# One-block sums over finished q and k rows, separate buffers for products and values, and softmax planned step by step

## The chip, the cores and the metric

The kernel runs on 1 core of one Trainium2 chip. The metric is the device time of one execution in microseconds, as the median of several runs.

## The reference, cut to what matters

With one sequence of 2048 positions and width 640, the output is x plus two branches of the same layernormed x: a local attention and a gated bilinear layer.

```python
xn = layernorm(x)                                   # no gain, eps 1e-5
# A: 32 heads of 20; each position sees itself and 7 earlier ones, 2 apart
qkv = xn @ wqkv                                     # q, k, v
logits[h, s, w] = q[h, s] . k[h, s - 2 * w] * 20 ** -0.5   # -1e9 where s < 2 * w
o[h, s] = sum_w softmax_w(logits)[h, s, w] * v[h, s - 2 * w]
A = o @ wo
# B
B = ((xn @ w_gate) * (xn @ w_up)) @ w_down          # inner width 1536
return x + A + B
```

Everything is bfloat16 in memory.

## The kernel before, in words

The 2048 positions are 16 tiles of 128, in 4 chunks of 512 (`CH` = 4 tiles each). The kernel is written as steps. `add(engine, cost, fn, deps, occ, after)` records a step with a planned cost; `Plan.order` then sorts all of them by list scheduling: among the steps that are ready on an engine it takes the one with the least latest-start time, and it moves the clock of that engine on by `occ`. The order that comes out is the order in which the instructions of each engine are issued. On the chip each engine works through its own queue strictly in that order and waits by semaphores. The plan's times are estimates written into the code by hand; on the chip nothing but the order is left of them.

For a chunk, the stages are:

- Layernorm of a tile: statistics on VectorE (DVE), the power on GpSimd (POOL), and the application on DVE, or from tile 8 on on ScalarE (ACT). The tile is transposed into `xnT`, from tile 4 on by a DMA transpose that is issued on SyncE's queue (SP, L353).
- `qk`: q and k of the chunk, transposed, by TensorE (PE, L419) and copied out of PSUM by ACT (L426). q and k have two buffers each, by chunk. A k tile has 14 columns in front, the last ones of the chunk before, which `halo` copies.
- `vproj`: v of each tile (L452), copied out by ACT and stored to a DRAM buffer `vD` by POOL's queue.
- `products` (L520): DVE multiplies q with the eight shifted k, in 8 instructions of 128x2560 for each chunk, in two halves of 256 positions. The 20 elements of a head lie on 4 partitions times 5 rows (`KT` = 5).
- `fold` (L496): DVE adds the 5 rows together. `LEVELS` = (1, 2, 3, 3) says how far in each chunk: with one level three rows are left, with two levels two, with three levels one. `logits` (L539) adds what is left over the 4 partitions on PE, with a small 0/1 matrix `Ek`: 12, 8, 4 and 4 matmuls for each half of the chunks 0 to 3. In this kernel the logits of both halves come after all products and folds of the chunk.
- The logits go out of PSUM by ACT (L555) and are transposed to `LT` by a DMA transpose on SP's queue (L562).
- `softmax`: one step `mx` on DVE (three maxima and a subtract, L581 to L585), the exponential on ACT (L590), and one step `nrm` on DVE (three sums, a reciprocal and a scale, L598 to L603), for each half.
- `load_v8` (L613): a DMA on SP's queue brings, for one tile, the eight shifted v rows of each position, 1280 KB. `av`: DVE multiplies them with the softmax (L638) and adds them in three tree instructions (L647, L651, L653) to `o`, which a DMA transpose on SP's queue (L660) turns into `oT`.
- `glu`: 24 groups of 5 matmuls (L680), ACT copies (L685) and a DVE product (L696) into `hT`.
- `down`: for each tile the matmuls over `hT` and `wd` (L740) and over `oT` and `wo` (L743), the copy out, and the store onto an output that already holds x. The first tile of a chunk does 10 of its 12 `hT` matmuls before it needs the last two.

PE gets the main matmuls in a written order (`pe_main`): for each chunk c the gate and up matmuls of c, `down` of c, then q, k and v of chunk c + 2. Only the logits groups are placed into it by the planner; they are marked urgent, and `margin` is the slack that the plan leaves between the last fold and them.

Products and v rows share one set of 5 buffers, tag `pv`. The order of the v loads on SP's queue is partly fixed in `load_v8`: in chunks 1 to 3 the second and third load of a chunk come behind the `LT` transposes of both halves (`SS`), and the first one behind the third product pair:

```python
order = [SPLAST[0]] if t < CH - 1 else [SS[2 * (t // CH) + 1]] if t % CH in (1, 2) else []
c, u = divmod(t, CH)
order.append(V8[t - 1] if u else PW[8 * c + 6])
```

Of the kernel before, what the change touches and what calls it, by code (L numbers as in the profile page):

```python
# [10 lines left out]
ALU = mybir.AluOpType  # L11
# [20 lines left out]
class Plan:  # L32


    LAG = 0.06
    INORDER = ("DVE", "PE", "ACT")
# [4 lines left out]
    def add(self, eng, cost, fn, deps=(), occ=None, after=(), kb=0):  # L41
        s = Step(eng, cost, fn, deps, occ, after)
        s.kb = kb
        s.idx = len(self.steps)
        self.steps.append(s)
        return s

    def order(self):
# [16 lines left out]
        while True:  # L65
            best = None
            for eng, items in ready.items():
                if not items:
                    continue
                f = free.get(eng, 0.0)  # L70
                t0 = max(f, min(r for r, _ in items))
                r, s = min((x for x in items if x[0] <= t0 + 1e-9), key=lambda x: (x[1].late, x[1].idx))
                if best is None or t0 < best[0]:
                    best = (t0, r, s)
            if best is None:
                break
            t0, r, s = best
            ready[s.eng].remove((r, s))
            s.start, s.end = t0, max(t0 + s.cost, s.floor)
            if s.kb:  # L80
                s.end = queue[s.eng] = max(t0 + 2.0, queue.get(s.eng, 0.0)) + s.kb / 340
                s.end = queue[s.eng] = max(s.end, s.floor)
            free[s.eng] = t0 + s.occ
            out.append(s)
            for t in s.succ:
                t.left -= 1
                if t.left == 0:
                    at = max(
                        d.start + d.occ if d in t.after else (d.start + d.occ if d.eng == t.eng and d.eng in self.INORDER else d.end + (0.0 if d.eng == t.eng else self.LAG) + t.margin)
                        for d in t.deps  # L90
                    )
                    ready.setdefault(t.eng, []).append((at, t))
# [5 lines left out]
def kernel(  # L98
# [296 lines left out]
    Q, Kk, LASTPW = {}, {}, {}  # L395
    HALOCP = {}

    def halo(c):
# [6 lines left out]
        if c == 0:  # L405
            HALOCP[c] = add("DVE", 0.1, fn)
        else:
            HALOCP[c] = add("ACT", 0.25, fn, [LASTPW.get(c - 2), *Kk[c - 1]])

    def qk(c, lo, n, rs=(0, 1)):  # L410
        for r in rs:
            for j in range(KT):
# [17 lines left out]
                mine = [WK if r else WQ, *[TX.get(t, TT[t]) for t in ts], LASTPW.get(c - 2)]  # L430
# [50 lines left out]
    PW, LL, LE, SS, DD, AA, O16, OE, V8, DT = {}, {}, {}, {}, {}, {}, {}, {}, {}, {}  # L481

    LEVELS = (1, 2, 3, 3)
    FOLDER = ('DVE', 'DVE', 'DVE', 'DVE')
    LEFT = (tuple(range(KT)), (0, 1, KT - 1), (0, KT - 1), (0,))
    HALVES = ((0, 2, 2, 4), (0, 1, 1, 2), (0, 1, KT - 1, KT))

    HS = CS // 2

    def fold(c, u):  # L490
        s = PW[8 * c + 2 * u + 1]
        for lo, hi, a, b in HALVES[: LEVELS[c]]:
            def fn(lo=lo, hi=hi, a=a, b=b):
                w = T["pw", c, u]
                if FOLDER[c] == "DVE":
                    nc.vector.tensor_tensor(w[:, :, lo:hi, :], w[:, :, lo:hi, :], w[:, :, a:b, :], ALU.add)  # L496
                else:
                    nc.gpsimd.dma_start(out=w[:, :, lo:hi, :], in_=w[:, :, a:b, :], accum_op=ALU.add)
            n = (hi - lo) * 4 * HS
            if FOLDER[c] == "DVE":  # L500
                s = add("DVE", 0.25 + n / 1920, fn, [s], occ=0.1 + n / 1920)
            else:
                s = add("POOL", 6.2, fn, [s], occ=1.2)
        return s

    def products(c, hf):
        for j in range(4):
# [15 lines left out]
            w = [LL.get(2 * c - 1), O16.get(4 * c - 4), O16.get(4 * c - 3), O16.get(4 * c - 2)][u]  # L523
            PW[m] = add("DVE", 1.48, mul, [*Q[c], *Kk[c], w], occ=1.395, after=[(FO[4 * c + 1] if i == 4 else PW.get(m - 1)) if i else V8.get(4 * c - 1)])
            if j % 2:
                FO[4 * c + u] = fold(c, u)
        LASTPW[c] = PW[m]
# [3 lines left out]
    def logits(c, g):  # L531
        n = 2 * c + g

        def lg():
            l = new(("lps", c, g), [P, 512], F32, "pl", 2, psum)
            left = LEFT[LEVELS[c]]
            for i in left:
                for j in range(4):
                    nc.tensor.matmul(l[H * j : H * (j + 1), :], lhsT=Ek[:], rhs=T["pw", c, 2 * g + j // 2][:, 2 * (j % 2) : 2 * (j % 2) + 2, i, :],  # L539
                                     start=(i == left[0]), stop=(i == left[-1]), tile_position=(0, H * j),  # L540
                                     skip_group_check=True)

        alone = not (g and c in PAIRED)
        took = 0.022 + 0.2195 * len(LEFT[LEVELS[c]]) + (0.19 if alone else 0.0)
# [30 lines left out]
    def softmax(c, hf):  # L575
        n = 2 * c + hf

        def mx():
            L4 = T["LT", n]
            m = sb.tile([P, 2, 4, H], BF, name="m", tag="m", bufs=1)  # L580
            nc.vector.tensor_tensor(m[:], L4[:, :, 0:4, :], L4[:, :, 4:8, :], ALU.max)  # L581
            nc.vector.tensor_tensor(m[:, :, 0:2, :], m[:, :, 0:2, :], m[:, :, 2:4, :], ALU.max)
            nc.vector.tensor_tensor(m[:, :, 0:1, :], m[:, :, 0:1, :], m[:, :, 1:2, :], ALU.max)
            d = new(("d", n), [P, 2, W, H], F32, "d", 2)
            nc.vector.tensor_tensor(d[:], L4[:], m[:, :, 0:1, :].to_broadcast([P, 2, W, H]), ALU.subtract)  # L585

        DD[n] = add("DVE", 1.52, mx, [SS[n], AA.get(n - 2)], occ=1.43)
# [7 lines left out]
        def nrm():  # L595
            d = T["d", n]
            s = sb.tile([P, 2, 4, H], F32, name="s", tag="s", bufs=1)
            nc.vector.tensor_tensor(s[:], d[:, :, 0:4, :], d[:, :, 4:8, :], ALU.add)  # L598
            nc.vector.tensor_tensor(s[:, :, 0:2, :], s[:, :, 0:2, :], s[:, :, 2:4, :], ALU.add)
            nc.vector.tensor_tensor(s[:, :, 0:1, :], s[:, :, 0:1, :], s[:, :, 1:2, :], ALU.add)  # L600
            nc.vector.reciprocal(s[:, :, 0, :], s[:, :, 0, :])
            a = new(("a", n), [P, 2, W, H], BF, "a", 2)
            nc.vector.tensor_tensor(a[:], d[:], s[:, :, 0:1, :].to_broadcast([P, 2, W, H]), ALU.mult)  # L603

        AA[n] = add("DVE", 2.33, nrm, [e, O16.get(2 * n - 3)], occ=2.24)

    def load_v8(t):
        def fn():
            v = new(("v8", t), [P, W, D], BF, "pv", 5)
# [21 lines left out]
    def av(t):  # L631
# [17 lines left out]
        def tree2():  # L649
            v = T["v8", t]  # L650
            nc.vector.tensor_tensor(v[:, 0:2, :], v[:, 0:2, :], v[:, 2:4, :], ALU.add)  # L651
            o = new(("o", t), [P, D], BF, "o", 2)
# [9 lines left out]
        O16[t] = add("DVE", 1.35, tree2, [b, OE.get(t - 2)], occ=1.26)  # L662
# [247 lines left out]
```

## Time and profile before

| What | us |
|---|---|
| median of 3 runs (261.37 to 263.31) | 261.53 |
| the profiled execution, its own time | 261.25 |
| its span, first to last instruction | 259.5 |
| PE busy | 252.8 |
| DVE busy | 230.4 |
| ACT busy | 121.7 |
| SP's hardware DMA queue, share of the 16 DMA engines' span | 49.9% |

The table comes from the profile page of one execution. A busy share is an average over stages that have different limits, so it doesn't tell by itself which engine a stage waits for; the lists of waits and the timelines do. In a timeline a row joins instructions of one line that follow each other; its first number is its start, the second its length. Matmuls overlap, so the step from one start to the next is what a group of matmuls costs the queue, and it is less than the row's length. The time of a DMA is from its issue to its landing. The line numbers L are those of the kernel before.

### The profile page before, as it was taken

The numbers are of one execution on the slowest core, as the hardware profiler recorded it, in microseconds if no ns is written. First come the engines' busy times: TensorE is split into PE (matmuls) and PEld (weight loads), VectorE is DVE, ScalarE is ACT, GpSimd is POOL, SyncE is SP. The second block draws the span as 40 slices with busy tenths as digits, with TensorE's granted clock in tenths as the row PEclk, the third lists the DMA queues.
The fourth block names the chain that finished last, engine by engine and source line by source line (L and its number), as shares of the span: only waits on it lengthen the run. The fifth ranks groups of instructions, "written<-read, shape, count | busy, mean of one in ns | idle before, by whom it ended". The sixth has DMA issues, their size and how long they took to land.

```text
span 259.5 us, 3922 instructions
## 1 busy us (share of the span) xinstructions
PE 252.8 (97%) x1451; PEld 141.7 (55%) x1470; DVE 230.4 (89%) x336; ACT 121.7 (47%) x233; POOL 48.5 (19%) x85
## 2 busy tenths in 40 slices
PE   7999999999999999999999989999999999999995
PEld 2655554444676646444467745644457754445763
DVE  5684998999999999799999995999999976999961
ACT  2757566856321457675521156465541136654100
POOL 4552004201042115800222110200031120000110
PEclk9999999999999999999999999999999999999999
DMA  7989994999989604991168925971157236951251
GB/s 219 344 176 237 399 376 125 418 334 247 294 161 254 109 20 130 361 265 27 25 150 155 206 34 155 371 240 25 25 144 207 31 31 148 370 177 24 28 78 51
DMA packets 51507, 46.54 MB, mean 179 GB/s; under 512 B 24626, under 2 KB 49472, under 8 KB 51424
## 3 DMA queue, kind: packets, MB, share of 16 engines
q1 hardware_dynamic: 46704, 37.10, 49.9%
q0 software_dynamic: 3184, 8.05, 15.2%
q10 hardware_dynamic: 1600, 1.15, 1.4%
q8 instruction: 11, 0.18, 0.3%
q14 instruction: 8, 0.07, 0.1%
HBM read 35.39 MB, written 7.55 MB: 165 GB/s over the span
## 4 chain that ended last, share of the span: by engine, by line
PE 54%; DVE 39%; issue 2%; POOL 2%; DMA 1%; ACT 1%; DVEq 0%; ACTq 0%; POOLq 0%
PE ps L680 20%; PE ps L419 11%; PE ps L740 10%; DVE pv L520 9%; DVE pv L638 7%; PE ps L452 6%; DVE pv L496 6%; PE ps L743 4%; DVE pv L647 4%; DVE hT L696 3%; DVE pv L651 2%; PE ps L242 2%; POOL ns L312 1%; DVE st L251 1%; DMA LT<-L 1%
## 5 line engine op out<-in xcount | busy, mean ns | idle before, releaser
L680 PE MATMUL ps<-xnT,wg 128*128 128x512 bf16 x230 | 59.1, 379 | 0.9 <-ACT v_t L458 0.4
L680 PE MATMUL ps<-xnT,wu 128*128 128x512 bf16 x238 | 59.5, 379 | 0.1
L740 PE MATMUL ps<-wd,hT 128*128 128x320 bf16 (+2 forms) x383 | 57.3, 299 | 0.1
L520 DVE TENSOR_TENSOR pv<-q,k 128x2560 bf16<-128x2560 bf16 x32 | 46.0, 1485 | 3.4 <-ACT k L426 3.4
L740 PEld LDWEIGHTS <-hT 128*128 128x128 bf16 x384 | 37.2, 98 | 15.8
L638 DVE TENSOR_TENSOR pv<-pv,a 128x5120 bf16<-128x5120 bf16 x16 | 45.1, 2819 | 0.1
L680 PEld LDWEIGHTS <-wu 128*128 128x128 bf16 x240 | 23.5, 98 | 28.3
L680 PEld LDWEIGHTS <-wg 128*128 128x128 bf16 x240 | 23.2, 98 | 28.7 <-issue 1.6
L685 ACT CAST us<-ps 128x512 bf16<-128x512 f32 x48 | 28.3, 590 | 18.1 <-PE ps L680 17.1
L685 ACT CAST gs<-ps 128x512 bf16<-128x512 f32 x48 | 28.3, 589 | 17.9 <-PE ps L680 17.8
L755 ACT COPY y<-ps 128x320 f32<-128x320 f32 x28 | 11.5, 426 | 53.0 <-PE ps L743 32.5
L496 DVE TENSOR_TENSOR pv<-pv 128x1024 bf16<-128x1024 bf16 (+1 forms) x36 | 31.7, 922 | 0.3
L743 PE MATMUL ps<-wo,oT 128*128 128x320 bf16 (+2 forms) x160 | 27.0, 299 | 0.3 <-DMA oT<-o 0.3
L784 POOL DMA_DIRECT2D out_dram<-y x14 | 12.3, 878 | 78.6 <-ACT y L755 78.6
L647 DVE TENSOR_TENSOR pv<-pv 128x2560 bf16<-128x2560 bf16 x16 | 23.8, 1486 | 0.1
L452 PE MATMUL ps<-wv,xnT 128*128 128x320 bf16 x160 | 23.3, 300 | 0.4 <-ACT xnT L365 0.4
L696 DVE TENSOR_TENSOR hT<-gs,us 128x512 bf16<-128x512 bf16 x48 | 19.6, 418 | 3.8 <-ACT us L685 3.8
L419 PE MATMUL ps<-xnT,wk 128*128 128x512 bf16 x98 | 22.6, 380 | 0.1
L419 PE MATMUL ps<-xnT,wq 128*128 128x512 bf16 x96 | 22.2, 379 | 0.2
L452 PEld LDWEIGHTS <-xnT 128*128 128x128 bf16 x160 | 15.3, 98 | 7.4 <-ACT xnT L365 0.6
L743 PEld LDWEIGHTS <-oT 128*128 128x128 bf16 x160 | 15.4, 98 | 6.9 <-DMA oT<-o 0.7
L419 PEld LDWEIGHTS <-wk 128*128 128x128 bf16 x100 | 11.5, 118 | 10.3 <-issue 1.1
(60 smaller groups left out, 198.2 us busy)
## 6 DMA issues: line engine op xcount, KB each, us to landing
pv<-vD SPq DMA_DIRECT2D x16, 1280.0 KB, 9.1
vD<-v_t POOLq DMA_DIRECT2D x16, 160.0 KB, 5.2
out_dram<-y POOLq DMA_DIRECT2D x14, 160.0 KB, 3.8
wg<-in_B_w_gate_dram SPq DMA_DIRECT2D x1, 1920.0 KB, 7.7
wu<-in_B_w_up_dram SPq DMA_DIRECT2D x1, 1920.0 KB, 12.0
wd<-in_B_w_down_dram SPq DMA_DIRECT2D x1, 1920.0 KB, 12.3
out_dram<-in_A_x_dram POOLq DMA_DIRECT2D x3, 640.0 KB, 6.5
x<-in_A_x_dram SPq DMA_DIRECT2D x11, 160.0 KB, 5.7
```

What stands on the lines that cost most here:

```text
L419: nc.tensor.matmul(T[key][:, 0:n], lhsT=(wk if r else wq)[:, i, :].rearrange("p (c b) -> p c b", b=KT)[:, :, j], rhs=T["xnT", c][:, i, lo ...
L452: nc.tensor.matmul(T["psv", t, n][:, 0:NS], lhsT=T["xnT", c][:, i, q * P : (q + 1) * P], rhs=wv[:, i, n * NS : (n + 1) * NS], start=(i == ...
L496: nc.vector.tensor_tensor(w[:, :, lo:hi, :], w[:, :, lo:hi, :], w[:, :, a:b, :], ALU.add)
L520: nc.vector.tensor_tensor(o, qh, kh, ALU.mult)
L638: nc.vector.tensor_tensor(v[:].rearrange("p w (j h) -> p w j h", j=Dh, h=H), v[:].rearrange("p w (j h) -> p w j h", j=Dh, h=H), T["a", n][ ...
L647: nc.vector.tensor_tensor(v[:, 0:4, :], v[:, 0:4, :], v[:, 4:8, :], ALU.add)
L680: nc.tensor.matmul(ps[:], lhsT=(wu if r else wg)[:, i, f * P : (f + 1) * P], rhs=T["xnT", c][:, i, :], start=(i == 0), stop=(i == KT - 1))
L685: nc.scalar.copy(s[:], T[key][:])
L696: nc.vector.tensor_tensor(h[:], T["gs", c, f][:], T["us", c, f][:], ALU.mult)
L740: nc.tensor.matmul(ps, lhsT=T["hT", c, f][:, q * P : (q + 1) * P], rhs=wd[:, f, sl], start=(f == 0), stop=(f == FT - 1 and not wo_part))
L743: nc.tensor.matmul(ps, lhsT=T["oT", t][:, g, :], rhs=wo[:, g, sl], start=False, stop=(g == KT - 1 and f1 == FT))
L784: nc.gpsimd.dma_start(out=out_flat[t * P : (t + 1) * P, :], in_=T["y", t][:], accum_op=ALU.add)
```

## The change

It has four parts.

1. In the chunks 1 to 3 `fold` goes down to one row, and the last of its three adds writes its result not into the product buffer but over rows of q or k that the products have used up: the first half's sums go to the first 256 columns of k and of q, the second half's to the next 256. `logits` reads them there, 4 matmuls for each half. Chunk 0 keeps one level and 12 matmuls. A new chunk's q and k now wait for the last logits of the chunk that used the buffer (`LL`), not for its last product.
2. Products have a tag of their own with 2 buffers, `pw`, and the v rows one with 3 buffers, `v8` (of which the second half of chunk 0's products borrows two). A v load of tile t waits for the `o` of tile t - 3. The loads lose the order behind the `LT` transposes; the first load of a chunk is ordered behind the `oT` transpose of the tile before.
3. The products of a half come as four steps and its folds behind them, each level a step; the softmax is planned as single instructions (`small`), and so are the last two tree adds of `av`.
4. The planner counts 0.116 us between two dependent DVE steps, and a long DVE step (over 0.6) gives way to a more urgent one that is ready within 0.12 us.

```diff
+    RAW = 0.116
...
+    def after_end(self, d, t):
+        if d in t.after:
+            return d.start + d.occ
+        if d.eng == t.eng and d.eng in self.INORDER:
+            return d.start + d.occ + (self.RAW if d.eng == "DVE" else 0.0)
+        return d.end + (0.0 if d.eng == t.eng else self.LAG) + t.margin
...
+                if eng == "DVE" and s.occ > 0.6:
+                    near = min((x for x in items if x[0] <= t0 + 0.12), key=lambda x: (x[1].late, x[1].idx))
+                    if near[1] is not s:
+                        r, s = near
+                        t0 = max(f, r)
...
-    LEVELS = (1, 2, 3, 3)
+    FIRST = 1
+    LEFT = (tuple(range(KT)), (0, 1, KT - 1), (0, KT - 1))[FIRST]
+
+    def summed(c, u):
+        if c == 0:
+            return [T["pw", 0, u][:, :, i, :] for i in LEFT]
+        lo = (u // 2) * HS
+        return [T["k" if u % 2 == 0 else "q", c][:, 0:4, lo : lo + HS]]
...
+        def last():
+            w = T["pw", c, u]
+            nc.vector.tensor_tensor(summed(c, u)[0], w[:, :, 0, :], w[:, :, KT - 1, :], ALU.add)
+
+        s = add("DVE", 1.22, level(0, 2, 2, 4), [s], occ=1.14)
+        if c == 0 and FIRST == 1:
+            return s
+        s = add("DVE", 0.69, level(0, 1, 1, 2), [s], occ=0.61)
+        if c == 0:
+            return s
+        return add("DVE", 0.69, last, [s, PW[8 * c + 4 * (u // 2) + 3]], occ=0.61)
...
-                    new(("pw", c, u), [P, 4, KT, HS], BF, "pv", 5)
+                    new(("pw", c, u), [P, 4, KT, HS], BF, *(("v8", 3) if c == 0 and hf else ("pw", 2)))
...
-            w = [LL.get(2 * c - 1), O16.get(4 * c - 4), O16.get(4 * c - 3), O16.get(4 * c - 2)][u]
+            w = None if c == 0 else LL[0] if c == 1 and hf == 0 else FO[4 * c + u - 2]
...
-        LL[n].margin = 0.9 if alone else 0.0
+        LL[n].margin = (0.9 if c == 0 else 2) if alone else 0.0
...
+        def small(op, occ, deps):
+            return add("DVE", occ + 0.083, op, deps, occ=occ)
...
-            v = new(("v8", t), [P, W, D], BF, "pv", 5)
+            v = new(("v8", t), [P, W, D], BF, "v8", 3)
...
-        order = [SPLAST[0]] if t < CH - 1 else [SS[2 * (t // CH) + 1]] if t % CH in (1, 2) else []
-        c, u = divmod(t, CH)
-        order.append(V8[t - 1] if u else PW[8 * c + 6])
+        order = [SPLAST[0]] if t < CH - 1 else []
+        if t:
+            order.append(V8[t - 1])
+        else:
+            order.append(PW[6])
         if t == 3:
             order.append(WL["o"])
-        w = LL[2 * c + (u - 1) // 2] if u else O16.get(t - 1)
+        if t >= CH and t % CH == 0:
+            order.append(OE[t - 1])
+        w = LL[1] if t in (1, 2) else O16.get(t - 3)
```

More of the change, by code (lines that the diff above doesn't have):

```diff
@@ L87, in order @@
                 if t.left == 0:
[L88 to L91, printed above, removed]
+                    at = max(self.after_end(d, t) for d in t.deps)
                     ready.setdefault(t.eng, []).append((at, t))
@@ L522, in products @@
             m = 8 * c + i
-            w = [LL.get(2 * c - 1), O16.get(4 * c - 4), O16.get(4 * c - 3), O16.get(4 * c - 2)][u]
[L524 to L527, printed above, removed]
+            w = None if c == 0 else LL[0] if c == 1 and hf == 0 else FO[4 * c + u - 2]
+            PW[m] = add("DVE", 1.48, mul, [*Q[c], *Kk[c], w], occ=1.395, after=[PW.get(m - 1)])
+        for u in (2 * hf, 2 * hf + 1):
+            FO[4 * c + u] = fold(c, u)
     PAIRED = ()
@@ L576, in softmax, with tree_step, op, sub @@
         n = 2 * c + hf
[L578 to L583, printed above, removed]
[L584 to L587 removed]
+        M = {}
+        def small(op, occ, deps):
+            return add("DVE", occ + 0.083, op, deps, occ=occ)
+        def tree_step(k, lo, src, alu):
+            def op():
+                if lo == 4:
+                    M[k] = sb.tile([P, 2, 4, H], F32 if k == "s" else BF, name=k, tag=k, bufs=1)
+                a = T[src, n] if lo == 4 else M[k]
+                nc.vector.tensor_tensor(M[k][:, :, 0:lo, :], a[:, :, 0:lo, :], a[:, :, lo : 2 * lo, :], alu)
+            return op
+        def sub():
+            d = new(("d", n), [P, 2, W, H], F32, "d", 2)
+            nc.vector.tensor_tensor(d[:], T["LT", n][:], M["m"][:, :, 0:1, :].to_broadcast([P, 2, W, H]), ALU.subtract)
+        a = [SS[n], AA.get(n - 2)]
+        for lo, occ in ((4, 0.21), (2, 0.143), (1, 0.11)):
+            a = [small(tree_step("m", lo, "LT", ALU.max), occ, [*a, DD.get(n - 1)])]
+        DD[n] = small(sub, 0.609, a)
         def ex():
```

61 lines of the change are left out of this document (26 added, 35 removed).

## The prediction

> **What bounds the kernel now.** I read the page first, then the list of waits by engine, then the timelines of PE, DVE and of SP's queue around chunks 1 and 2. From the page:
>
> ```profile
> span 259.5 us, 3922 instructions
> PE 252.8 (97%) x1451; PEld 141.7 (55%) x1470; DVE 230.4 (89%) x336; ACT 121.7 (47%) x233; POOL 48.5 (19%) x85
> ...
> PEclk9999999999999999999999999999999999999999
> DMA  7989994999989604991168925971157236951251
> ```
>
> From the list of PE's waits, all of them:
>
> ```profile
> PE ps L242 <- DVE wv L192: 1.3, 1, 1.3
> PE pl L539 <- DVE pv L496: 0.6, 1, 0.6
> PE ps L680 <- ACT v_t L458: 0.4, 1, 0.4
> PE ps L452 <- ACT xnT L365: 0.4, 1, 0.4
> PE ps L743 <- DMA oT<-o: 0.3, 1, 0.3
> ```
>
> TensorE has work from end to end at the full clock; after its start it waits 1.7 us in all. So PE's own queue sets the time. The chain that ended last runs over DVE from 42 to 153 us, but it ends there in a PE wait of 0.63 us, so DVE is only just in time. Two things can move the time: PE work that goes, and lateness somewhere else that makes PE wait. A change to DVE or to DMAs can hardly gain, and can lose.
>
> The profiled execution took 261.25 us: its span of 259.5 and 1.75 around it. The median of the runs is 261.53, 0.28 above; I sum against 261.25 and add 0.28.
>
> **What PE gains.** Timeline of PE:
>
> ```profile
> 93.20 0.62 PE L539 MATMUL pl<-pv,Ek 128*32 128x512 bf16 x8
> 93.75 3.43 PE L419 MATMUL ps<-xnT,wk 128*128 128x512 bf16 x14
> ...
> 149.14 3.40 PE L419 MATMUL ps<-xnT,wq 128*128 128x512 bf16 x14
> 153.17 0.40 PE L539 MATMUL pl<-pv,Ek 128*32 128x512 bf16 x4 [0.63 <-DVE pv L496]
> 153.50 2.35 PE L419 MATMUL ps<-xnT,wq 128*128 128x512 bf16 x10
> ```
>
> The starts count: a logits group of 8 matmuls holds the queue from 93.20 to 93.75 (0.55 us), one of 4 from 153.17 to 153.50 (0.33). Chunk 1 now sums to one block like chunks 2 and 3: two groups fall from 8 to 4 matmuls, 2 x 0.22 = 0.44 gained. That the right operand now lies in q and k rows changes neither count nor size; 0. The 0.63 wait goes, as chunk 2's first sums are now ready 1 to 2 us before PE reaches them (laid out as below). The 0.40 wait goes: ACT's copies of v stood behind layernorm applications that waited for POOL, and in the new order these come after the copies. The 0.34 wait for oT stays or grows. So PE without new waits: 261.25 - 0.44 - 0.63 - 0.40 = **259.78**. This is nearly the floor.
>
> **DVE.** Added: four last sums in chunk 1 (1024 elements, 684 ns long, one every 0.61 if independent, 0.69 if it needs the one before), about 2.5 us. Saved: softmax steps planned singly can stand between others; a maximum costs 0.33, 0.26, 0.23 start to start when each needs the one before, and 0.21, 0.15, 0.11 with something between. I laid the new DVE order out from 42.06 (the first maximum) with such spacings from the DVE timeline: product 1.40, subtract 0.61, the three sums and reciprocal 0.45, 0.32, 0.26, 0.59, scale 0.61 (0.72 before its multiply), multiply 2.73, trees 1.40, 0.75, 0.41 (0.08 more each when it needs the one before), gate product 0.34, folds 1.14 and 0.61. This gives the o of tile 1 at 68.2 (before 65.4), of tile 2 at 74.2 (71.8), of tile 3 at 77.0; the first half's sums of chunk 1 are ready at 86.1; PE reaches its logits (now after one q group) at 86.63 + 1.08 = 87.7. In time. Four products (91.8) and one fold bring DVE to **92.95**, and the next in its queue is the maximum of LT(1,0), with the rest of the second half's folds behind it.
>
> **The DMAs of SP's queue.** The three v loads of 1280 KB stood behind both LT transposes in chunks 1 to 3; now, with three slots of their own, they are issued right after the oT transpose of the chunk's last tile, ahead of LT, and in chunk 2 also ahead of the last three xnT transposes of chunk 3. SP's timeline before:
>
> ```profile
> 74.36 1.23 SPq L353 DMA_TRANSPOSE xnT<-x  x1
> 77.46 1.20 SPq L660 DMA_TRANSPOSE oT<-o  x1
> 78.75 0.53 SPq L613 DMA_DIRECT2D pv<-vD  x1
> 94.50 5.79 SPq L562 DMA_TRANSPOSE LT<-L  x2
> 100.46 2.36 SPq L613 DMA_DIRECT2D pv<-vD  x3
> 108.87 20.07 SPq L660 DMA_TRANSPOSE oT<-o  x3
> ```
>
> Asked for the three loads from 100 us on, and for the transpose at 108.87, the trace gives time to landing:
>
> ```profile
> DMA to landing us min/median/max: 6.1/10.7/15.0
> ...
> DMA to landing us min/median/max: 8.6/8.6/8.6
> ```
>
> So the loads (issued at 100.46, 101.02, 101.74) landed at 106.5, 111.7, 116.8: 5.1 us apart. At 158 and 217 us the same triple landed 3.5 to 4.6 apart; the mean of six gaps is 4.26. The transpose behind them landed at 117.4, 0.7 us after the last load, where LT at 94.50 with nothing in front took 2.4. The same holds for oT at 54.69 (0.7 after the load in front) and at 65.41 (2.3 after). So a transpose issued behind loads comes when they are done.
>
> Chunk 1. The first load landed at 87.57 before, behind the same transposes; I keep that. The third: 87.57 + 2 x 4.26 = 96.1; LT(1,0), issued at about 88.7, lands at 96.8. DVE waits from 92.95, **3.85 us**. Behind the waiting maximum stand the folds of the second half: their last sum, 103.1 without the wait, comes at 106.9. PE reaches those logits (now after the first gate group) at 104.20 - 0.22 + 1.08 - 0.55 = 104.5. **PE waits 2.4.** DVE stays 3.85 behind: gate products of chunk 1 keep their distance to PE (the tenth is due on PE at 133.4, ready at 131.5).
>
> Chunk 2. The o of chunk 1's last tile, 131.4 without the delay, comes at 135.25. Its transpose takes 1.23 to issue, then the three loads go at 136.5; the first lands 6.1 later (5.9 to 6.2 in three cases), the third at 136.5 + 6.1 + 8.5 = 151.1; behind it three xnT transposes: 0.7 and two more at 0.55 (xnT at 140.89 and 141.44 before): 152.9. PE's first q group of chunk 3 needs all of them; it began at 149.14, and would now at 149.14 - 0.40 - 0.44 + 0.33 (chunk 2's first logits now stand before it) + 2.4 = 151.0. **PE waits 1.9.** In chunk 3 PE is then 4.3 late and DVE 3.85, and loads issued at 193 are down by 206, before LT is issued; no third wait.
>
> **Sum:** 259.78 + 2.4 + 1.9 = 264.1; **264.4** as a median.
>
> **Bounds.** Gap between loads 3.5 to 5.2, transposes 0.7 to 2.3 behind. At the low end LT lands at 95.3, PE waits 0.9 and then 0.3: 261.0, 261.3 as a median. At the high end the third load is at 98.0, LT at 100.3: 5.9, then 5.3: 271. I take the mean gap, as POOL's stores run beside part of these loads as they did at 101 to 117. Writing sums into rows with q's and k's stride: no row; by the products, which read k with that stride at 1.40 for 2560, nothing; at worst a sum at twice its 0.61, 12 x 0.61 = 7.3 on DVE over three chunks, of which some 2 us would reach PE in each. I take nothing.
>
> The Trainium skill, DMA: Bandwidth & Descriptors, Queues, rings and completion order, says that each DMA engine takes descriptors in ring order, but that completion over the 16 engines is not first-in first-out for one issuing engine. By its second half a transpose could be down before the last load, and the time would be the first rival's; the three landings above speak against it here.
>
> **Rivals.**
> A (not slower): the loads clear in time. LT is issued 10 us after the first load, and xnT some 3 us after theirs; if landings don't queue (LT at 88.7 + 2.4 = 91.1, before 92.95) nothing is late. For it: the page's DMA digits are 6 and 0 tenths in the slices 84 to 91 and 91 to 97, so there is room. Against: the three late transposes. It decides if the third load lands before 92.2. Time 259.8 + 0.3 = 260.1.
> B: only oT of tile 2. Tile 1's o is now planned behind the next multiply (2.73), so SP issues its transpose at 68.2, not 65.4, and the four xnT and oT of tile 2 behind it; this oT is then the fifth transpose in that run, and the fifth landed at 81.0 before. PE is there at 78.67: waits 2.3 in place of 0.34. Time 262.1. In my forecast this wait comes earlier on the same queue and is covered by the 2.4 (PE arrives late anyway), so it isn't added.
> C: DVE becomes the bound through slow sums on strided rows: 2 us or more in chunks 1 to 3 beyond A: 266.
>
> **How the numbers follow.** Forecast 0.55, A 0.22, B 0.15, C 0.08. Range 260.0 to 267.5: A at its edge, the forecast up to a gap of 4.8. What a measurement of this kernel can tell from no change is about 1%, 2.6 us. Faster by that needs 258.9, below PE's floor: 0.03. Slower by that, over 264.15: over half of the forecast and all of C, with some of B's mixtures: 0.42. The rest, 0.55, within.
>
> **What would show it.** PE's waits: none at L539 in chunk 2, one of 1 to 4 us at chunk 1's second logits (released by DVE), one at chunk 3's first q group (by DMA xnT), perhaps one at the output projection for oT of tile 2. DVE's wait for LT in chunk 1 about 4 us. SP: three v loads before LT, LT of chunk 1 taking 6 to 9 us to land instead of 2.4. The forecast is wrong if LT lands in about 2.4 us there, if PE waits elsewhere, or if the new sums are longer than 0.7 us.

## The result, and the profile after

The changed kernel takes 277.44 us (median of 4 runs, 276.23 to 278.51), the kernel before 261.45 beside it. The ratio is 1.060, with a 95% interval of 1.054 to 1.066. It is slower by 16 us, and 10 us beyond the upper end of the forecast's range. The profiled execution is the one of 278.51 us.

The page of the changed kernel, the same rows as before and the row of VectorE:

```profile
span 276.8 us, 3898 instructions
PE 256.4 (93%) x1444; PEld 142.1 (51%) x1462; DVE 229.1 (83%) x340; ACT 119.0 (43%) x233; POOL 69.9 (25%) x85
...
DVE  5776996999999759999999819999999939999311
...
PEclk9999999999999999999999979999999999999899
```

TensorE's share fell from 97% to 93%, and two slices show a lower clock (7 and 8 tenths), which the kernel before has nowhere; that is also why PE counts as busy for longer (256.4 against 252.8 us) with less to do. VectorE is busy for about as long as before (229.1 against 230.4 us). What stands out is GpSimd: 69.9 us against 48.5, with as many instructions.

The large ones of PE's waits in the changed kernel (total, times, longest):

```profile
PE ps L429 <- DMA xnT<-x: 5.3, 1, 5.3
PE ps L777 <- DVE hT L733: 4.2, 2, 3.1
PE ps L780 <- DMA oT<-o: 2.2, 1, 2.2
PE pl L558 <- DVE k L515: 1.6, 1, 1.6
...
PE ps L717 <- ACT y L792: 1.2, 1, 1.2
```

In order of time, with the small ones that follow them in the same list: hT 1.1 and oT of tile 2 2.2 in chunk 0, k and q rows (the new one-block sums) 1.6 + 0.2 at chunk 1's second logits, xnT 5.3 + 0.2 at chunk 3's first q group, y 1.2 and hT 3.1 in chunk 3. That is 15.0 us beside the 1.3 and 0.4 of the start. Behind the two waits of 5.3 and 3.1 the granted clock in the records is 0.5 for 3.41 us each, from 159.19 and from 254.76; in the kernel before it is full from 6.81, where its records begin, to 259.39, the last 0.1 us of the span. While it lasts PE does half as much, so the two cost up to 3.4 us more. The prediction had 259.78 for PE without new waits, with 0.34 for oT in it: 259.78 - 0.34 + 15.0 + 3.4 = 277.8, against 278.51.

Where the first of these waits come from shows on SP's queue (its timeline in chunk 1; start, time to issue):

```profile
79.27 1.30 SPq L696 DMA_TRANSPOSE oT<-o  x1
80.66 4.90 SPq L642 DMA_DIRECT2D v<-vD  x3
92.25 1.78 SPq L580 DMA_TRANSPOSE LT<-L  x1
```

The three loads are issued ahead of LT, as forecast. They landed at 89.11, 94.69 and 99.44, and LT behind them at 99.83, 7.6 us after its issue. VectorE waited 4.99 us for it.

Where the last ones come from shows in chunk 3. First GpSimd's timeline, then VectorE's over the same time, then the one row of ACT's waits that belongs to it:

```profile
200.81 18.96 POOL L758 COPY gate<-hT 1x1 bf16<-1x1 bf16 x1 [21.60 <-DVE hT L733]
219.71 0.52 POOL L751 DMA_DIRECT2D out_dram<-in_A_x_dram  x1
220.23 1.11 POOL L745 DMA_DIRECT2D x<-in_A_x_dram  x2
221.32 1.85 POOL L821 DMA_DIRECT2D out_dram<-y  x2
```

```profile
210.96 5.69 DVE L539 TENSOR_TENSOR pw<-q,k 128x2560 bf16<-128x2560 bf16 x4
216.57 2.96 DVE L510 TENSOR_TENSOR pw<-pw 128x2048 bf16<-128x2048 bf16 x3
219.44 0.28 DVE L605 TENSOR_TENSOR m<-LT 128x256 bf16<-128x256 bf16 x1
219.76 0.45 DVE L605 TENSOR_TENSOR m<-m 128x128 bf16<-128x128 bf16 x2
```

```profile
ACT y L792 <- DMA out_dram<-y: 19.0, 3, 12.2
```

The gate is a copy of one element, 0.38 us at its shortest here. It took 18.96. It ended (219.77) within 0.05 us of the end of the first maximum (219.725), at VectorE's first pause since 188.5: the next maximum needs the first and starts 0.035 us after it has ended, while up to then each instruction starts some 0.08 us before its predecessor's end. Behind the gate on GpSimd's queue stand the seed copy, two loads and the y stores. Without the stores ACT has no y slot, and it stood for 12.2 us (to 226.18); behind its y copies stood an exponential, for which VectorE waited 4.75 us (to 227.50), and PE felt both.

From this came the theories to be tried. Theory 1: the loads ahead of the transposes. Theory 2: VectorE's rows of two-input instructions without a pause keep GpSimd out of SBUF, and what waits behind it on its queue comes late. A smaller third: the order of VectorE's work in chunk 0, which makes o of tile 1 late.

### The profile page after: what moved, and what is told of

Its sections match the earlier page's. It is cut to its first block, busy times and chain, and to the rows that moved or that the text cites. A ratio compares the mean times of both kernels' runs of the same rounds, so it can differ in the third digit from the quotient of the medians.

```text
span 276.8 us, 3898 instructions
## 1 busy us (share of the span) xinstructions
PE 256.4 (93%) x1444; PEld 142.1 (51%) x1462; DVE 229.1 (83%) x340; ACT 119.0 (43%) x233; POOL 69.9 (25%) x85
## 4 chain that ended last, share of the span: by engine, by line
DVE 33%; PE 17%; issue 10%; DMA 10%; POOL 3%; ACT 1%; SPq 0%; POOLq 0%; DVEq 0%; ACTq 0%
DVE v L671 12%; PE ps L777 6%; DVE v L680 5%; PE ps L429 5%; DMA LT<-L 4%; DVE hT L733 4%; PE ps L780 3%; DVE v L684 3%; DMA xnT<-x 2%; PE ps L462 2%; DMA oT<-o 2%; DMA out_dram<-y 2%; DVE s L605 2%; DVE o L689 2%; POOL rstd L275 1%
## 5 line engine op out<-in xcount | busy, mean ns | idle before, releaser
L777 PE MATMUL ps<-wd,hT 128*128 128x320 bf16 (+2 forms) x383 | 58.6, 302 | 4.3 <-DVE hT L733 4.2
L671 DVE TENSOR_TENSOR v<-v,a 128x5120 bf16<-128x5120 bf16 x16 | 45.1, 2819 | 0.1
L539 DVE TENSOR_TENSOR pw<-q,k 128x2560 bf16<-128x2560 bf16 x28 | 40.1, 1484 | 3.5 <-ACT k L436 3.5
L758 POOL COPY gate<-hT 1x1 bf16<-1x1 bf16 x3 | 19.9, 6640 | 47.4 <-DVE hT L733 47.4
L780 PE MATMUL ps<-wo,oT 128*128 128x320 bf16 (+2 forms) x160 | 27.7, 305 | 2.2 <-DMA oT<-o 2.2
L429 PE MATMUL ps<-xnT,wq 128*128 128x512 bf16 x96 | 23.5, 395 | 5.7 <-DMA xnT<-x 5.3
L510 DVE TENSOR_TENSOR pw<-pw 128x2048 bf16<-128x2048 bf16 (+1 forms) x26 | 24.1, 972 | 0.0
L680 DVE TENSOR_TENSOR v<-v 128x2560 bf16<-128x2560 bf16 x16 | 23.8, 1485 | 0.1
L483 POOL DMA_DIRECT2D vD<-v_t x16 | 9.1, 571 | 48.6 <-ACT v_t L468 48.3
```

The lines of the kernel that those rows point to most:

```text
L429: nc.tensor.matmul(T[key][:, 0:n], lhsT=(wk if r else wq)[:, i, :].rearrange("p (c b) -> p c b", b=KT)[:, :, j], rhs=T["xnT", c][:, i, lo ...
L539: nc.vector.tensor_tensor(o, qh, kh, ALU.mult)
L671: nc.vector.tensor_tensor(v[:].rearrange("p w (j h) -> p w j h", j=Dh, h=H), v[:].rearrange("p w (j h) -> p w j h", j=Dh, h=H), T["a", n][ ...
L680: nc.vector.tensor_tensor(v[:, 0:4, :], v[:, 0:4, :], v[:, 4:8, :], ALU.add)
L758: nc.gpsimd.tensor_copy(g[0:1, 0:1], T["hT", c - 1, SEED_AT][0:1, 0:1])
L777: nc.tensor.matmul(ps, lhsT=T["hT", c, f][:, q * P : (q + 1) * P], rhs=wd[:, f, sl], start=(f == 0), stop=(f == FT - 1 and not wo_part))
```

## The experiments

**The loads put back.** Only SP's queue is altered: in the finished order of all steps, nine load steps are moved.

```diff
+    for c, behind_ in ((1, SS[2]), (2, SS[4]), (3, SS[6])):
+        for t in (c * CH + 2, c * CH + 1, c * CH):
+            seq.remove(V8[t])
+            seq.insert(seq.index(behind_) + 1, V8[t])
```

> The changed kernel (277.4 us) with nothing altered but SP's queue: the three v loads of chunks 1, 2 and 3 are issued behind the first LT transpose of their chunk (in chunk 2 also behind the last three xnT transposes) instead of ahead of them. Every other engine's order is the same. Theory 1 (the loads ahead of the transposes are what PE waits for): LT(1,0) lands 1.5 to 3 us after its issue instead of 7.6, PE's waits at chunk 1's second logits (1.6 + 0.2) and for xnT (5.3) go, and with the second the slow clock behind it (3.4 us at half speed, 1.7 us): 277.4 - 8.8 = 268.6. Theory 2 (GpSimd is kept from running by VectorE's rows of tensor_tensor, and its queue of DMAs with it): the gate copy of chunk 3 stays at 10 us or more, ns of tiles 13 to 15 stay late, so most of the xnT wait stays (xnT is issued late for want of ns): 273 to 276.

Measured: 271.93 us (271.52 to 273.78), 5.5 less. LT landed 3.1 us after its issue. The wait at chunk 1's second logits is gone, and the one for xnT in chunk 3's first q group as well, although ns of tiles 13 to 15 is as late as it was (5.92 us for three instructions, 5.93 in the changed kernel). So the 5.3 us belong to the loads, and what I had put against theory 2 in this expectation, that late ns would keep xnT late, is wrong. The gate of chunk 3 stayed at 18.96 us, and PE's wait for y in chunk 3 grew to 4.1, with 6.83 us of half clock behind it. That is the main reason why less came off than the 8.8 expected.

**GpSimd given two pauses.** A chain of ten dependent tiny additions on VectorE, behind the last layernorm statistics and behind the hT product that releases the gate.

```diff
+    def pause():
+        g = sb.tile([P, 16], F32, name="gap", tag="gap", bufs=1)
+        nc.vector.memset(g[:, 0:1], 0.0)
+        for n in range(10):
+            nc.vector.tensor_scalar(g[:, n + 1 : n + 2], g[:, n : n + 1], scalar1=EPS, scalar2=None, op0=ALU.add)
```

> The changed kernel with nothing altered but two pauses on VectorE: a chain of ten tiny additions, each needing the one before (about 1.5 us), behind the last layernorm statistics (tile 15) and behind the hT product that the gate of chunk 3 waits for. Theory 2: in the pauses GpSimd gets through, so the gate copy takes under 2 us instead of 19.0, rstd and ns of tiles 13 to 15 are done within 2 us of the last ve instead of 9, ACT's wait for y slots (12.2) goes and with it PE's waits of 1.2 and 3.1 in chunk 3 and the slow clock behind the second; the xnT wait falls from 5.3 to 2 to 3 (loads still in front): 277.4 - 6.0 - 3 to 5 = 266.5 to 268.5. Theory 1 alone: the gate and ns are long because of something else or do not matter; VectorE has 3 us more to do, so 277 to 279.

Measured: 275.16 us (274.02 to 278.3), 2.3 less. GpSimd's timeline of this kernel:

```profile
139.78 1.59 POOL L277 TENSOR_TENSOR rstd<-ve,mhalf 128x1 f32<-128x1 f32 x3 [4.96 <-DVE ve L269]
141.38 0.73 POOL L330 TENSOR_SCALAR ns<-mv,rstd 128x1 f32<-128x1 f32 x3
201.94 0.18 POOL L768 COPY gate<-hT 1x1 bf16<-1x1 bf16 x1 [19.34 <-DVE gap L282]
```

The six layernorm instructions took 2.3 us instead of 9.7, and the gate 0.18 instead of 18.96. PE's waits for y and for hT in chunk 3 are gone. So GpSimd runs when VectorE pauses. But the time went elsewhere. The wait for xnT did not fall to 2 to 3 us; it is 6.5, with 6.83 us of half clock behind it, and oT of tile 2 was waited for 3.1 us, with 3.41 behind it. The xnT transposes were ready to be issued at once, and the queue did not take them: SP's timeline has

```profile
141.46 2.33 SPq L650 DMA_DIRECT2D v<-vD  x3
143.84 13.59 SPq L371 DMA_TRANSPOSE xnT<-x  x3
```

The first of the three took 9.1 us to issue (143.84 to 152.95), where one takes 1.2 to 1.3 us on a free queue; the loads in front landed at 147.85, 154.23 and 157.66. Behind loads, being early with ns buys nothing.

**Both.** The two edits together.

> Both edits together: the v loads behind the first LT of their chunk, and the two pauses on VectorE. If the two theories name all that is large: 277.4 - 8.8 - 6.0 = 262.6, with PE's waits for oT of tile 2 (2.2) and for chunk 0's hT (1.1) left, and a bit above the kernel before (261.5). If the order in which VectorE's work is planned costs something else in chunks 1 to 3, it stays above 266.

Measured: 266.2 us (265.32 to 268.16), a ratio of 1.017 [1.012, 1.022] to the kernel before. That is just on the far side of the 266 given: the order of VectorE's work costs something besides. What was left of PE's waits was 3.2 us for oT of tile 2 (with 3.41 us of half clock behind it) and 1.8 for hT in chunk 2. The two theories are 11.2 of the 16 us, more than the 5.5 and 2.3 that each edit took off alone: alone, each had let another wait grow (for y, and for xnT).

**The port by itself.** Ten rows of VectorE instructions, with three tiny GpSimd instructions in each.

```diff
+    def prod(k):
+        nc.vector.tensor_tensor(big[:, k, :], p1[:], p2[:], ALU.mult)
...
+        for k in range(count):
+            op(k)
+            if k == 1:
+                for m in range(3):
+                    nc.gpsimd.tensor_copy(gt[0:1, 4 * r + 4 + m : 4 * r + 5 + m], second())
```

> No attention or GLU is computed (the output is a copy of x with 48 values of the probe's own): ten rows of VectorE operations, and in each row three tiny GpSimd operations back to back, released by the end of the row's second VectorE operation. Rows: (0) 14 independent bf16 products 128x2560, two inputs; (1) the same, each reading the one before; (2) 36 independent products 128x512; (3) 14 one-input multiplications by a constant; (4) 6 fp32 products 128x1280; (5) 14 products with a broadcast operand; (6) as 0 with two tiny dependent additions after the seventh; (7) products 128x2560 and 128x512 in turn; (8) as 0 with GpSimd memsets; (9) as 0 with GpSimd tensor_scalar 128x1 as ns is. Theory 2 (GpSimd is starved over many operations): in rows 0, 2 and 7 the first GpSimd copy lasts several products, up to the row's end (5 to 17 us); in row 1 each ends at the next bubble (up to 1.5 us each); in row 6 it ends at the dependent additions (some 7 us). A lock per operation: every copy ends with the VectorE operation under way, 0.3 to 1.5 us each in rows 0, 1, 5, 6, 7 and under 0.5 in row 2. No contention: 0.1 to 0.4 us each in all rows. Rows 3 and 4 should be free of it by all three if only two-input operations in the fast mode hold the port.

GpSimd's timeline of the probe (start, sum of the group):

```profile
26.12 17.05 POOL L122 COPY gt<-big 1x1 bf16<-1x1 bf16 x3 [25.67 <-DVE big L85]
46.41 3.03 POOL L122 COPY gt<-big 1x1 bf16<-1x1 bf16 x3 [3.23 <-DVE big L88]
...
78.96 9.04 POOL L122 COPY gt<-big 1x1 bf16<-1x1 bf16 x3 [1.77 <-DVE big L94]
91.11 5.83 POOL L122 CAST gt<-fb 1x1 bf16<-1x1 f32 x3 [3.11 <-DVE fb L97]
...
120.19 7.23 POOL L122 COPY gt<-big 1x1 bf16<-1x1 bf16 x3 [3.11 <-DVE big L85]
...
165.15 0.16 POOL L126 MEMSET big<- 1x1 bf16 x3 [3.17 <-DVE big L85]
165.37 16.53 POOL L130 COPY gt<-big 1x3 bf16<-1x3 bf16 x1
```

These are the rows 0, 1, 3, 4, 6 and 8. In row 0 the first copy lasted 16.8 us, over all twelve products that were left, and ended (42.93) 0.05 us after the last of them; the two behind it took 0.18 each. Where each product reads the one before (row 1) two of the three took 1.5 us, one product each, and one 0.18. Two dependent additions in the middle of the row (row 6) ended the wait there, after 7.0 us; the copy ended (127.19) before the first addition did (127.20), so here it was not the pause between the two that let it in; the change from a product to a tiny one-input addition was enough. A row of short products (11.4 us), products in turn (22.6 us), a broadcast operand (16.8) and a tensor_scalar on GpSimd (16.9) all went like row 0. A memset took 0.09, and the copy behind it in the same row again 16.5. So the copy is not kept out for one instruction alone: that it ends with the operation under way, after 1.5 us, is true of row 1 only. Wrong was the expectation for rows 3 and 4: one-input multiplications by a constant kept the copy out for 8.8 us and fp32 products for 5.6, to the row's end in both.

The Trainium skill, SBUF — State Buffer, Who interferes with whom, says that a VectorE instruction with two SBUF inputs contends with a GpSimd instruction that reads SBUF, not with one that only writes it; the 16.8 and 0.09 us agree. It also says, in its Summary: rules for kernel authors, that the one that issues second is blocked until the first has ended. The measurement goes further: in these rows it stays blocked over the next ones too, for as long as they follow without a pause.

**A gate that reads nothing.** VectorE writes one element behind the hT product, and GpSimd's gate writes it again.

```diff
-            nc.gpsimd.tensor_copy(g[0:1, 0:1], T["hT", c - 1, SEED_AT][0:1, 0:1])
+            nc.gpsimd.memset(T["gate", c][0:1, 0:1], 0.0)
```

> The changed kernel (277.4 us) with another gate for the seed copies: VectorE writes one element of a tile of its own behind the hT product, and GpSimd's gate is a memset of that element, so it waits for the same instruction but reads no SBUF; rstd and ns stay as they are. In the probe a memset took 0.09 us where a copy waited 16.8. If the read is what starved GpSimd and the gate what cost chunk 3: gate 0.1 to 0.3 us instead of 19.0, ACT's wait for y slots and PE's 1.2 and 3.1 in chunk 3 gone with the slow clock behind the second, all else as it is: 277.4 - 6.0 = 271.4. If VectorE or the queue of DMAs is what is late in chunk 3: 275 to 278.

Measured: 273.02 us (272.48 to 274.82), 4.4 less. The gate of chunk 3 on GpSimd's timeline, where 18.96 us stood:

```profile
199.70 0.09 POOL L759 MEMSET gate<- 1x1 bf16 x1 [20.94 <-DVE gate L735]
```

The stores flowed, and PE's waits for y and hT in chunk 3 and the half clock there went. 1.6 us less came off than expected: 0.7 + 0.2 of waits at chunk 3's second logits came in their place, and oT of tile 2 was waited for 2.5 us, now with 3.41 us of half clock behind it, and the half clock behind the xnT wait (4.9 us) lasted 6.83 us instead of 3.41.

**o of tile 1 early.** One VectorE instruction moved ahead of tile 2's multiplication.

```diff
+    seq.remove(O16[1])
+    seq.insert(seq.index(B2[1]) + 1, O16[1])
```

> The changed kernel (277.4 us) with one VectorE instruction moved: the last tree step of chunk 0's tile 1, which makes o, stands ahead of tile 2's multiplication by a (2.8 us) again, as in the kernel before. Covered (what the prediction assumed): the wait for oT of tile 2 (2.2 us) goes, and most of the one for hT in chunk 0 (1.1), but LT(1,0) still lands at about 99.8 us behind the loads, so the wait at chunk 1's second logits grows from 1.8 by as much as PE comes earlier, to 4 to 5 us, and being over 3 us it draws the slow clock behind it: 277 to 279. Not covered: the 3.3 us come off, 274.

Measured: 274.25 us (270.74 to 274.81), 3.2 less, the time given for "not covered". The profiled execution is the fastest of the four, 270.74, and in it the gate of chunk 3 took 0.38 us, although the program's gate and row are the same. So part of that run's gain is chance; that the gate was long in the other three, which agree within 0.8 us, is likely and not shown. What the profile does show is chunk 0: the waits there fell from 1.1 + 2.2 to 0.4 + 1.2, 1.8 of the 3.2, and the waits at chunk 1's logits stayed, 1.5 + 0.2 against 1.6 + 0.2, at a time 2.0 us earlier. SP issued the loads 1.25 us earlier (79.41 against 80.66), and LT landed at 97.87 instead of 99.83. Not all of that is the edit: chunk 0's first LT, which the edit doesn't touch, landed at 41.84 here and at 43.13 in the changed kernel's profile. In the two other kernels with o late and the loads ahead (GpSimd given two pauses, and the gate that reads nothing) that LT landed at 41.88 and 42.02; against them the loads went out 0.6 to 1.0 us earlier here, and chunk 1's LT landed 0.95 to 2.05 earlier.

**The three edits.** Loads back, gate that reads nothing, o of tile 1 early; no pauses.

> The changed kernel with three edits: the v loads behind the first LT of their chunk, the gate that reads nothing, and o of tile 1 ahead of tile 2's multiplication; no pauses on VectorE. rstd and ns of tiles 13 to 15 stay slow. If the three name all of the loss: PE without new waits is 259.8 + 0.3, and with the 0.4 for xnT that is already in it and waits of up to 1 us for hT it gives 260 to 262, no slower than the kernel before (261.5 to 261.9). If something of the new planning still costs: above 264.

Measured: 262.27 us (10 runs, 261.67 to 263.7), a ratio of 1.0034 [1.0011, 1.0057]. Of the 16 us that the change costs, these three edits take back 15.2. It is 0.3 above the 262 given. The two largest of PE's waits in this kernel after the start:

```profile
PE pl L558 <- DVE q L515: 0.8, 1, 0.8
PE ps L784 <- DMA oT<-o: 0.6, 1, 0.6
```

The clock is full throughout. rstd and ns are still slow (3.73 and 5.93 us) and cost nothing that can be seen. That leaves 0.85 us to the kernel before.

**The planning undone.** The old planner and grouped steps, with the new blocks and slots.

```diff
-        DD[n] = small(sub, 0.609, a)
+        DD[n] = add("DVE", 1.52, mx, [SS[n], AA.get(n - 2)], occ=1.43)
...
-        b = add("DVE", 0.82, tree2, [b], occ=0.74)
-        O16[t] = add("DVE", 0.49, tree3, [b, OE.get(t - 2)], occ=0.41)
+        O16[t] = add("DVE", 1.35, tree2, [b, OE.get(t - 2)], occ=1.26)
```

> The changed kernel with the planning part undone: softmax's maxima and sums and the last two tree steps are one step each as before, and the planner has neither the 0.116 us for a dependent VectorE operation nor the look for a nearby more urgent one; the one-block sums, the rows they are written over and the own slots stay. If planning the steps singly is what makes VectorE's rows without a pause: the gate of chunk 3 is under 3 us, o of tile 1 is early, and only the loads' waits are left (1.8 and 5.3, and the slow clock behind the second): 267 to 269. If the rows come from the slots and the order of the products: the gate stays over 10 us, and the time at 274 to 278.

Measured: 267.32 us (267.26 to 267.65), in the range given for the planning. The gates of chunks 2 and 3 took 1.38 us each, and chunk 0 has no wait, as expected. The waits that are left are in part others than expected, so that the time fits so well is partly luck: at chunk 1's second logits PE waited 1.5 + 0.2, as in the changed kernel, but with 3.41 us of half clock behind it; at chunk 3's first q group it waited 3.0 for ACT's y copies, at full clock, in place of 5.3 for xnT; and at chunk 3's second logits 1.1.

**The planning undone, and the loads put back.** The edits of the first and of the last experiment.

> The changed kernel with the planning part undone (267.3 us) and the v loads of chunks 1 to 3 issued behind the first LT of their chunk. If the loads are all that the one-block sums and the own slots cost: PE's wait at chunk 1's second logits (1.5 + 0.2) and the slow clock of 3.4 us behind it go, 267.3 - 3.4 = 263.9, and with the wait of 3.0 that ACT's y copies make at chunk 3's first q group (y stores behind the loads) 261. If that last wait has another cause, such as ns, it stays: 264.

Measured: 261.79 us (10 runs, 261.45 to 263.12), a ratio of 1.0007 [0.998, 1.003]. The waits at the logits are gone, and instead of ACT's 3.0 PE waited 1.9 for xnT. The profiled execution is the slowest of the ten, 263.12, and the only one with a half clock in it (3.41 us, behind that wait). So the one-block sums and the own slots by themselves cost and bring nothing beyond some 0.3%: it is where the loads stand that costs.

**The planning alone.** The kernel before with the new planner and single steps, and nothing else.

> The kernel before (261.4 us) with only the planning part of the change: softmax's maxima and sums and the last tree steps planned one by one, 0.116 us for a dependent VectorE operation, and the look for a nearby more urgent step. Slots, loads and sums as before. If the planning by itself is what delays o of tile 1 and packs VectorE's rows so that GpSimd is kept out: 264 to 270, with PE waiting for oT of tile 2 by 1 to 3 us or a gate over 5 us. If it costs only together with the loads ahead and the new slots: 260.5 to 263.

Measured: 264.48 us (264.43 to 265.8), a ratio of 1.012 [1.008, 1.016]. PE waited for oT of tile 2 by 1.8 us, and for another oT in chunk 3 by 1.3; the gates of chunks 2 and 3 took 5.92 and 2.85 us. So the planning costs something alone, by the late o rather than by the gate, as PE's list has no wait for y, and much less than in the new kernel.

Put together, these medians are a square (the kernel before took 261.4 to 261.9 beside them): new blocks with old planning 261.8 (loads behind) and 267.3 (loads ahead), with new planning 271.9 and 277.4. The loads cost 5.5 in both rows, the planning 10.1 in both columns, where it costs 3.0 on the kernel before. What goes with this is the length of VectorE's rows without a pause, worked out from the trace (a pause is where an instruction starts after its predecessor's end). The longest is 13.3 us in the kernel before, 14.7 with the planning alone, 20.0 with the blocks alone, and 31.2 in the changed kernel (188.5 to 219.7), with the gate in the middle of it. The time in rows of over 8 us is 51, 57, 74 and 135 us. The rows by themselves cost little: the kernel with the three edits has them as long (31.2 us at most, 133 us in rows over 8) and takes 262.3. They cost through what GpSimd has to read while they last, and through the late o: the gate that reads nothing and the early o take 9.7 us off the kernel with the loads put back (271.9), nearly all of the planning's 10.1.

**Two more moves.** On top of the three edits: the last sum of chunk 2's second half ahead of tile 8's multiplication, and the fourth xnT transpose of chunk 2 behind oT of tile 2.

```diff
+    seq.remove(FO[11])
+    seq.insert(seq.index(MU[8]), FO[11])
+    seq.remove(TT[11])
+    seq.insert(seq.index(OE[2]) + 1, TT[11])
```

> The kernel with the three edits (262.3 us) and two more moves in its order: the last sum of chunk 2's second half stands ahead of the multiplication of tile 8 on VectorE, so that PE's wait of 0.8 + 0.4 at those logits goes, and the fourth xnT transpose of chunk 2 stands behind oT of tile 2 on SP's queue, so that PE's 0.6 for oT goes: 262.3 - 1.8 = 260.5, and at most 1% faster than the kernel before (261.4). If xnT is then late instead, or the multiplication's delay of 0.6 reaches PE, 262 to 263.

Measured: 262.94 us (12 runs, 261.37 to 264.56), a ratio of 1.0043 [1.0019, 1.0068] to the kernel before: a miss. Both waits went, but hT was late by 0.7 in chunk 0 and by 0.4 and 1.2 in chunk 2. No kernel tried here beats the one before.

## Why the prediction was wrong, point by point

**What bounds the kernel; a change to DVE or DMAs can hardly gain and can lose: right.** Nearly all of the loss is PE waiting, and the clock that fell behind the longer waits.

**PE without new waits, 259.78: too low by about 1.** In the kernel with the three edits chunk 1's logits groups hold PE for 0.33 us instead of 0.55, as counted. But its span is 260.5 with 2.0 us of listed waits, so 258.5 without, where the same sum for the kernel before is 259.5 - 1.7 = 257.8. The 0.44 is not in the end; about 1.1 us lie in small pieces that no wait in the list accounts for; what they are stays open. The 0.63 at chunk 2's first logits went, as said, and so did the 0.40 for v_t.

**DVE's order from 42.06: o of tile 1 at 68.2 was measured at 70.5**, when its transpose is issued, and with it hT was 1.1 us late, which the prediction did not have. The 2.3 us are two waits ahead of it. The first maximum came at 43.15, 1.1 later than laid out, as chunk 0's first LT landed at 43.13; that is chance in part, for it landed at 41.6 to 43.0 in the seven other kernels that have the new blocks and the new planning. And up to 48.70 VectorE waited 1.23 us for ACT's copy into `us`; in front of that copy ACT had waited for GpSimd's ns, which took 1.55 us beside a VectorE product, where the next two took 0.26. This second wait is in all eight, most likely from GpSimd kept out once more.

**PE waits 2.4 at chunk 1's second logits: the mechanism is right, and the size came out near by two errors.** The first load landed at 89.11 instead of 87.57, the gap was 5.2 us, not 4.26, and LT came 0.4 behind the third (0.7 forecast): 99.83 instead of 96.8. But PE came later too, at 107.9 instead of 104.5, after 3.36 us of waits in chunk 0. 1.8 was measured, and 1.7 in the kernel with the planning undone, where chunk 0 has no waits.

**Rival B's wait, "covered by the 2.4, so it isn't added": this step failed.** That a late PE shortens the later wait is so as long as LT stands still: in the four kernels with the new planning and the loads ahead, the second half's first sum ended 9.56 to 9.57 us after LT landed, and in the one with the gate that reads nothing PE, held up by 2.5 us and a slow clock in chunk 0, waited only 0.2 at these logits. But the lateness that makes oT late also moves the loads and LT on the same queue. With o of tile 1 late the loads went out at 79.99 to 80.66 and LT landed at 98.82 to 99.92 (three kernels); with o early they went out at 79.25 and 79.41, and LT landed at 97.57 and 97.87 (the planning undone, and o early). So both waits stood, and with the one for hT chunk 0 cost 3.0 us beyond the 0.34. That B's 2.3 came out at 2.21 is luck: oT landed at 82.21 instead of 81.0, and PE was there at 80.04 instead of 78.67. B's time has a slip too: 259.78 holds 0.34 of this wait already, so 261.7, not 262.1.

**PE waits 1.9 at chunk 3's first q group: mis-sized, 5.3 measured.** The loads went out at 141.49 instead of 136.5 (5.0 later), landed 13.6 us after the first issue instead of 14.6, the last xnT came 4.3 behind them instead of 1.8, and PE was there at 154.28 instead of 151.0: 1.9 + 5.0 - 1.0 + 2.5 - 3.3 = 5.1. The term of 0.55 us for each further transpose was taken where no loads were in flight; here their issue took 2.1 to 3.5 us each. That the whole goes away with the loads is shown.

**"No third wait": this step failed most.** There were 1.2 and 3.1 us in chunk 3, and in both kernels where an edit made the gate short (two pauses, and the gate that reads nothing) these two are gone. It rested on DVE's and SP's queues alone. GpSimd's queue was counted with its transfers, and never with its own small instructions, of which the trace of before had a hint: its gate at 128.11 took 2.71 us, to the end of a VectorE multiplication of 2.82, against 0.71 at 189.32.

```profile
128.11 2.71 POOL L721 COPY gate<-hT 1x1 bf16<-1x1 bf16 x1 [17.92 <-DVE hT L696]
```

**The clock: not in the sum at all**, up to 3.4 us. **The upper end of the range** is above its own terms: each us of gap costs 4 us in that sum (two gaps in each of the two waits), so a gap of 4.8 gives 264.4 + 4 x 0.54 = 266.5, not 267.5; the 277.44 is far beyond either.

**Rival A: false**, LT landed behind the loads in all kernels that have them ahead. **Rival C: false.** The sums onto rows with q's and k's stride take 0.69 us, like the sums in a block of their own.

The corrections of the waits and the clock lead to 264.1 + 3.0 (chunk 0) - 0.6 + 3.7 (xnT) + 4.3 (chunk 3) + 3.4 (clock) = 277.9, against 278.51 of the profiled execution.

## What to carry to other kernels

When a change fills the pauses of VectorE, look for every GpSimd instruction that reads SBUF and has DMAs queued behind it: a copy of one element can last as long as the row of VectorE work it meets, where a memset in its place took 0.09 us here. Ask of every transfer moved ahead on a queue what is issued behind it, and price the issue as well as the landing. A wait that is found upstream is not covered by one downstream if the same lateness moves what the second one waits for.

## What the runs showed of the hardware that I had not expected

- A GpSimd instruction that reads SBUF can be kept out for a whole row of VectorE instructions: 16.8 us over twelve products in the probe, 18.96 us in the kernel. Rows of bf16 multiplications by a constant (8.8 us) and of fp32 products (5.6 us) do it too. A pause of 0.035 us between dependent instructions is enough to let it in (row 1 of the probe, and the end of the 18.96 us). In the full kernel one sometimes got in at a boundary without a pause: rstd and ns in chunk 2 took 0.6 to 2.5 us each among products and folds, and the same gate 0.38 us in one run and 18.96 in another. What decides there stays open.
- A DMA transpose takes 1.2 to 1.3 us to issue on a free queue. The first three xnT transposes behind three loads of 1280 KB took 2.0 to 9.1 us each. What makes them slow is not shown: LT transposes with one or two such loads still on the way took 1.2 to 2.2, and in the changed kernel one xnT transpose took 4.5 (135.56) with none of these loads on the way.
- The granted clock falls to 0.5 for stretches of 3.41 or 6.83 us. In these runs it did so after idle times of PE of 3.06 us and more, of 2.46, of 1.89, and of 1.51 with 0.21 close behind; it did not after 2.21, 2.35 and, once, 2.98, nor after 1.50 with 0.21 close behind in another kernel. The Trainium skill, TensorE: Matmul & The Clock Gate, Part 1: The HAM clock gate and Why this matters for your kernels, gives a window of 3413 ns for this and warns of idle times beyond some 3 us; the stretches agree with one or two windows, and here the length of the idle time alone does not decide.
